# Attention on one core: minima, block copy and fill eviction shifted at unit ends

## The chip, the core and the metric

The kernel runs on one core of a Trainium2 chip. The metric is the device time of one execution in microseconds (us); the median of several runs is compared. TensorE is called PE here, VectorE DVE, ScalarE ACT, GpSimd POOL, and SP is the engine whose queue issues the DMAs.

## The reference

```python
def reference(A_x, A_wqkv, A_wo, B_x, B_w_r, B_w_gate, B_w_up, B_w_down, gate_w):
    x = A_x                                    # 1 x 2048 x 512, fp32
    g = _sigmoid((x * gate_w).sum(-1, keepdims=True))
    # a: softmax attention, 32 heads of 16, all 2048 keys for each query
    qkv = (x @ wqkv) ...                       # q, k, v: 32 x 2048 x 16
    p = _softmax(einsum("bhqd,bhkd->bhqk", q, k) * 16 ** -0.5)
    a = einsum("bhqk,bhkd->bhqd", p, v) ... @ wo
    # b: the two tokens with the largest x @ w_r pass a SwiGLU of width 1792, are scaled by
    # sigmoid of their score and added to x; all other tokens stay
    b = x + upd
    return g * a + (1 - g) * b
```

Almost all of the time goes to attention: 32 x 2048 x 2048 scores, an exponential of each, and the product of the exponentials with V.

## The kernel before

**Units.** The work is cut into 32 units. A unit is two heads and 1024 queries (the last four: four heads and 512 queries). Its scores are computed transposed, 128 keys at a time: 16 steps of four pieces, `s_piece`, each a matmul of 128 keys by 512 queries into a bank of the ring `st` (three banks), followed by an exponential on ACT into the tile `P`. Two steps later `av_mm` multiplies `P[s]` with V (the "P V" of a step, `A` in the order) and accumulates the unit's block in one PSUM bank, `av`. That bank exists once. After a unit's sixteenth step `av_out` copies it to SBUF (tile `o`, on ACT, line 670), and SP sends it off in eight DMAs.

**Maxima.** The softmax needs each query's maximum over all keys ahead of its scores. So PE computes the scores a second time, some 21 steps earlier, with queries on partitions: `m_piece`, 64 pieces for a unit, each a matmul (line 576). DVE reduces them (line 580). Of three successive pieces the first two share the two-bank tile `mxa` and one reduction, and the third has `mxb`; each tile exists once, so PE can fill one only after DVE has reduced what stood in it. When a unit's 64 pieces are reduced, `m_unit` forms the minima of its negated maxima on DVE (tile `m`, line 623), POOL splits them into a high and a low part (`hl`, lines 77 and 78), and behind the next two-bank reduction `m_rows` transposes `hl` on DVE (`hr`, line 634) and sends it in eight small DMAs into two rows of the unit's `Qx`, where the score matmuls pick it up.

**Order.** Every engine works its instructions in the order in which the program issues them, and the order is written out by hand. A pattern covers three steps:

```python
ORDER = "sssmmA smssmmA msssmmf smssmmAm".replace(" ", "")
```

`s` is a piece of scores, `m` a piece of maxima, `A` a step's P V, and `f` a fill: one piece of other work for PE from a generator (projections of later heads' q and k, the SwiGLU, the output projection), collected in a bank `fl`. A fill's PSUM result isn't copied at once: it is put on the list `late`, and `run_late` empties the list at the start of the next pattern. Evictions of projections (`evict`, tile `pe`, line 188) are copied by ACT and then split by two POOL operations into `ev` (lines 190 and 191), which SP stores. Those of the output projection (`acc_add`, tile `w`, line 464) are added up by POOL.

A unit's 64 pieces of maxima are not a multiple of three. So the last piece of a unit u falls on the second piece of `mxa` where u % 3 is 1, on the first where u % 3 is 0 (it is reduced together with the next unit's first piece), and on `mxb` where u % 3 is 2. In the first two cases the minima follow a two-bank reduction, in the third a one-bank reduction. A pattern is three steps and a unit sixteen, so the P V of a unit's last step is the last `A` of a pattern where u % 3 is 0, the first where it is 1, and the second where it is 2.

**Small operations.** Other small DVE operations are queued in `gaps`, and unit minima that await their transpose in `turn`. Behind each two-bank reduction `m_piece` takes one thing, a transpose first.

Of the kernel before, what the change touches and what calls it, by code (L numbers as in the profile page):

```python
# [11 lines left out]
AF = mybir.ActivationFunctionType  # L12
# [8 lines left out]
UNITS = PAIRS * 2  # L21
KT = S // 128
VW = DH + 1
LEAD = 21
STEPS = UNITS * KT
EL = 64
# [10 lines left out]
def gated_mix(ctx: ExitStack, tc: tile.TileContext, xT, x, wqkv, wo, w_rg, w_gate, w_up, w_down,  # L37
              consts, pos, out):
    nc = tc.nc
# [10 lines left out]
    def st_tile(shape=(128, 512)):  # L50
        return psum.tile(list(shape), F32, tag="st", name="st", bufs=3)
# [4 lines left out]
    def mxa_tile():  # L56
        return psum.tile([128, 2, 512], F32, tag="mxa", name="mxa", bufs=1)

    def mxb_tile(shape=(128, 512)):
        return psum.tile(list(shape), F32, tag="mxb", name="mxb", bufs=1)  # L60
# [4 lines left out]
    def o_tile(name, shape, dt=F32):  # L65
        return ring.tile(shape, dt, tag="o", name=name, bufs=6)
# [9 lines left out]
    def pool_split(hi, lo, src):  # L76
        nc.gpsimd.tensor_scalar(hi, src, 1.0, None, op0=OP.mult)  # L77
        nc.gpsimd.tensor_sub(lo, src, hi.bitcast(F32))
# [102 lines left out]
    def run_late():  # L181
        for f, a in late:
            f(*a)
        late.clear()
# [77 lines left out]
    def k_of(u, c):  # L262

        return Kx[(u // 2) % 2 if u < QU else 2 * c]
# [299 lines left out]
    MX, P, AV = {}, {}, {}  # L564

    def m_piece(g):

        u, e = divmod(g, EL)
        t, c, j = e // 8, e // 2 % 4, e % 2
        r = g % 3  # L570
        if r == 0:
            MX[0] = mxa_tile()
        elif r == 2:
            MX[1] = mxb_tile()
        dst = MX[0][:, r] if r < 2 else MX[1]
        nc.tensor.matmul(dst, Qx[u % 3][64 * j:64 * j + 48, t * 128:t * 128 + 128],  # L576
                         k_of(u, t // 4)[64 * j:64 * j + 48, c * 512:c * 512 + 512], start=True, stop=True)
        if r:
            g0 = (g - 1 if r == 1 else g) % (3 * EL)
            nc.vector.tensor_reduce(Mr[:, g0:g0 + (2 if r == 1 else 1)], MX[r - 1], axis=AX.X, op=OP.max, negate=True)  # L580
            if r == 1:

                if turn:
                    m_rows(*turn.pop())
                elif e > 1 and e < EL - 1 and gaps:
                    gaps.pop(0)()
            if e == EL - 1 or (e == 0 and r == 1 and g):
                m_unit(u if e else u - 1)
                if u == UNITS - 1 and e:
                    m_rows(*turn.pop())  # L590
# [30 lines left out]
    def m_unit(u):  # L621
        m = ring.tile([128, 2, 8], F32, tag="m", name="m", bufs=2)
        nc.vector.tensor_reduce(m, Mr[:, EL * (u % 3):EL * (u % 3) + EL].rearrange("p (t c j) -> p j t c", c=4, j=2),  # L623
                                axis=AX.X, op=OP.min)
        hl = ring.tile([128, 2, 2, 8], F32R, tag="hl", name="hl", bufs=2)
        pool_split(hl[:, :, 0], hl[:, :, 1], m)
        turn.append((u, hl))

    turn, gaps = [], []

    def m_rows(u, hl):

        r = ring.tile([128, 32], F32R, tag="hr", name="hr", bufs=2)
        nc.vector.transpose(r.bitcast(F32), hl.rearrange("p j i t -> p (j i t)").bitcast(F32))
        for j in range(2):
            for b in range(4):
                q = Qx[u % 3][64 * j + 48:64 * j + 50, :].rearrange("i (t n) -> i t n", n=128)
                p0 = 32 * b + 16 * j
                nc.sync.dma_start(q[:, :, 32 * b:32 * b + 32].bitcast(F32), r[p0:p0 + 16, :].bitcast(F32))

    def s_piece(s, j, c):
        u, kt = divmod(s, KT)
        if s not in P:
            P[s] = ring.tile([128, 4, 512], F32, tag="P", name="P", bufs=3)
        k = k_of(u, c)[64 * j:64 * j + 50, kt * 128:kt * 128 + 128]
        q = Qx[u % 3][64 * j:64 * j + 50, c * 512:c * 512 + 512]
        ps = mxb_tile() if s > STEPS - LEAD and c == 1 and j == 0 else st_tile()
        nc.tensor.matmul(ps, k, q, start=True, stop=True)  # L648
        nc.scalar.activation(P[s][:, 2 * j + c, :], ps, AF.Exp)  # L649

    def av_mm(s):
        u, kt = divmod(s, KT)
        if kt == 0:
            AV[0] = av_tile()
        for ct in range(4):
            h = (u // 2 * 2 if u < QU else H - 4 + ct % 2 * 2) + ct // 2
            nc.tensor.matmul(AV[0][32 * ct:32 * ct + 32, :], V[:, kt, h * VW:h * VW + 32], P[s][:, ct, :],  # L657
                             start=kt == 0, stop=kt == KT - 1)
        del P[s]
# [1 line left out]
    Lt = {}  # L661

    def av_out(u):
        pair, half = divmod(u, 2)
        g, pp = divmod(pair, 4)
        o = o_tile("o", [128, 512])
        if STEPS > u * KT + KT + 2 > STEPS - LEAD:
            nc.vector.tensor_copy(o, AV[0])
        else:
            nc.scalar.activation(o, AV[0], AF.Copy)  # L670
        if u >= QU:
            AV[u] = o
            if u == UNITS - 1:
                return
            Ls = AV["l", u] = ring.tile([128, 16], F32, tag="Ls", name="Ls", bufs=2)
            for ct in range(4):
                p = 64 * (ct % 2) + 32 * (ct // 2)
                nc.sync.dma_start(Ls[p:p + 32, :], o[32 * ct + 16:32 * ct + 17, :])
            half, q = divmod(u - QU, 2)
            for ct in range(4):  # L680
                r = 64 + 32 * (ct % 2) + 16 * (ct // 2)
                nc.sync.dma_start(last_n[half][r:r + 16, q * 512:q * 512 + 512], o[32 * ct:32 * ct + 16, :])
            return
        if u % 8 == 0:
            Lt[g] = ring.tile([128, 128], F32, tag="Lt", name="Lt", bufs=1)
        for ct in range(4):
            j, c = divmod(ct, 2)
            q0 = c * 512
            r = pp * 32 + j * 16
            if g < 3:  # L690
                d = a_scr[g * 128 + r:g * 128 + r + 16, half * 1024 + q0:half * 1024 + q0 + 512]
            else:
                d = last_n[half][r:r + 16, q0:q0 + 512]
            nc.sync.dma_start(d, o[32 * ct:32 * ct + 16, :])
            p = r + half * 8 + c * 4
            nc.sync.dma_start(Lt[g][p:p + 4, :], o[32 * ct + 16:32 * ct + 17, :])
# [78 lines left out]
    def end_step(s):  # L775
        now[0] = s
        for f, a in fill.pop(s, []):
            f(*a)
# [113 lines left out]
    def start_step(s):  # L892
        now[0] = s
        u = s // KT + 2
        if s % KT == 0 and u < UNITS:
            if u % 2 == 0 and 2 < u <= QU:
                load_k(u // 2)
            load_q(u)

    count = dict(s=0, m=0, A=-2)  # L900

    def m_next():
        if count["m"] < UNITS * EL:
            m_piece(count["m"])
            count["m"] += 1
# [3 lines left out]
    def parts_next(n):  # L909
        for _ in range(n):  # L910
            next(parts, None)
# [9 lines left out]
    count["m"] = 4 * LEAD  # L921

    while count["m"] < UNITS * EL:
        run_late()
        for o in ORDER:
            if o == "s":
                s, i = divmod(count["s"], 4)
                if i == 0:
                    start_step(s)
                s_piece(s, i % 2, i // 2)  # L930
                count["s"] += 1
                if i == 3:
                    end_step(s)
            elif o == "m":
                m_next()
            elif o == "A":
                if count["A"] < 0:
                    parts_next(3)
                p_v(count["A"])
                count["A"] += 1  # L940
            else:
                next(fills, None)
    for s in range(count["s"] // 4, STEPS + 2):
        run_late()
        if s < STEPS:
            start_step(s)
            for i in range(4):
                s_piece(s, 1 - i % 2, i // 2)
        p_v(s - 2)
        next(fills, None)  # L950
        end_step(s)
# [34 lines left out]
```

## Time and profile before

| | |
|---|---|
| three runs, median (lowest to highest) | 1433.41 us (1433.03 to 1433.73) |
| the profiled execution: its own time | 1430.75 us |
| its span, first to last instruction | 1428.9 us |
| granted PE clock, of full speed | 0.999 |
| PE busy | 1417.6 us, 99% |
| DVE busy | 1292.6 us, 90% |
| ACT busy | 1169.4 us, 82% |
| POOL busy | 312.9 us, 22% |
| exponentials, `P<-st` (ACT, line 649) | 2028 of 599 ns |
| two-bank reductions (DVE, line 580) | 655 of 1216 ns |
| one-bank reductions (DVE, line 580) | 654 of 689 ns |

The profile is of one execution, whose own time is 1430.75 us; the span leaves out 1.85 us around it. Busy time of PE is modelled: a matmul's end is not observed, so a short wait of PE can look busy. A row of the timeline reads: start in us, duration in us, engine, line, operation, tile written <- tiles read, with partitions x elements, and the count of instructions merged into the row. Square brackets give the engine's idle time before the row and what ended it.

### The profile page before, as it was taken

Reading aid. Unit: us, or ns where it says so; the run is one execution under the profiler, and the core shown is the slowest. Engines: PE = TensorE matmul, PEld = TensorE weight load, DVE = VectorE, ACT = ScalarE, POOL = GpSimd, SP = SyncE. Lnnn points to the kernel's source line nnn. Section 1 sums busy time; section 2 is a strip of 40 time slices with the busy share of each in tenths; the row PEclk is TensorE's granted clock in tenths of the full one; section 3 lists DMA queues with packets and bytes.
Section 4 is the critical chain, followed back from the end, with each engine's and each line's share of the span. In section 5 each row is a group of like instructions: output and inputs, shape, how many; then the busy total and the mean of one; then the engine's idle time right before and its main releaser. Section 6 shows DMA issues by size and latency. Waiting matters only on the chain.

```text
span 1428.9 us, 24152 instructions
## 1 busy us (share of the span) xinstructions
PE 1417.6 (99%) x9113; PEld 628.9 (44%) x9113; DVE 1292.6 (90%) x1534; ACT 1169.4 (82%) x2262; POOL 312.9 (22%) x329
## 2 busy tenths in 40 slices
PE   9999999999999999999999999999999999999998
PEld 6654444444444444444444443434444444444433
DVE  5879999999999999999999999999999999999942
ACT  4468888888888888888888888888888888888886
POOL 3661100112000001200000100032742322234500
PEclk9999999999999999999999999999999999999999
DMA  8611021212214121312222332414313031012012
GB/s 261 183 56 49 20 53 31 54 45 43 53 52 109 62 53 31 68 29 57 65 82 53 85 84 77 106 41 134 83 31 68 21 77 35 15 31 58 17 50 78
DMA packets 55096, 92.87 MB, mean 65 GB/s; under 512 B 14208, under 2 KB 25472, under 8 KB 53476
## 3 DMA queue, kind: packets, MB, share of 16 engines
q1 hardware_dynamic: 54884, 91.32, 24.7%
q8 instruction: 72, 1.18, 0.4%
q14 instruction: 44, 0.36, 0.1%
q0 software_dynamic: 96, 0.01, 0.0%
HBM read 63.77 MB, written 28.57 MB: 65 GB/s over the span
## 4 chain that ended last, share of the span: by engine, by line
PE 97%; DMA 2%; SPq 0%; DVE 0%; ACT 0%; issue 0%; ACTq 0%; DVEq 0%
PE av L657 36%; PE st L648 24%; PE mxa L576 12%; PE mxb L576 10%; PE fl L154 6%; PE fl L498 4%; PE st L283 3%; DMA xs<-xT 1%; PE mxa L607 1%; DMA wvs<-wqkv 1%; PE fl L389 0%; PE st L154 0%; DMA k_scr<-Qx 0%; PE fl L427 0%; ACT P L649 0%; DVE acc L549 0%
## 5 line engine op out<-in xcount | busy, mean ns | idle before, releaser
L649 ACT ACTIVATE P<-st 128x512 f32<-128x512 f32 x2028 | 1064.4, 599 | 200.7 <-PE st L648 108.8
L580 DVE TENSOR_REDUCE Mr<-mxa 128x2 f32<-128x1024 f32 x655 | 796.6, 1216 | 3.9 <-PE mxa L576 3.0
L657 PE MATMUL av<-P,V 128*32 128x512 f32 x4096 | 545.3, 605 | 0.0
L648 PE MATMUL st<-Qx,Kx 50*128 50x512 f32 x2028 | 537.5, 443 | 1.8 <-ACT P L649 1.8
L580 DVE TENSOR_REDUCE Mr<-mxb 128x1 f32<-128x512 f32 x654 | 450.9, 689 | 62.6 <-PE st L648 20.6
L648 PEld LDWEIGHTS st<-Qx,Kx 50*128 50x128 f32 x2028 | 276.7, 184 | 232.3 <-ACT P L649 213.4
L576 PE MATMUL mxb<-Kx,Qx 48*128 48x512 f32 x654 | 325.3, 497 | 0.0
L576 PE MATMUL mxa<-Kx,Qx 48*128 48x512 f32 x1310 | 296.0, 418 | 0.0
L576 PEld LDWEIGHTS mxb<-Kx,Qx 48*128 48x128 f32 x654 | 119.5, 183 | 273.7 <-DVE Mr L580 271.2
L576 PEld LDWEIGHTS mxa<-Kx,Qx 48*128 48x128 f32 x1310 | 124.9, 183 | 46.5 <-DVE Mr L580 5.4
L657 PEld LDWEIGHTS av<-P,V 128*32 128x32 f32 x4096 | 81.1, 108 | 141.5 <-issue 135.3
L77 POOL TENSOR_SCALAR hl<-m 128x16 fp32r<-128x16 f32 x32 | 8.1, 255 | 434.3 <-DVE m L623 434.3
L190 POOL TENSOR_SCALAR ev<-pe 128x512 fp32r<-128x512 f32 x24 | 35.8, 1492 | 299.0 <-ACT pe L188 299.0
L465 POOL TENSOR_TENSOR acc<-acc,w 128x512 f32<-128x512 f32 x32 | 41.0, 1281 | 166.7 <-ACT w L464 152.4
L154 PE MATMUL fl<-xh,wh 128*128 128x512 f32 x96 | 42.9, 447 | 0.0
L154 PE MATMUL fl<-xh,wl 128*128 128x512 f32 x96 | 40.4, 421 | 0.0
L549 DVE SCALAR_TENSOR_TENSOR acc<-fl,gg,acc 128x512 f32<-128x512 f32 x16 | 12.0, 748 | 26.3 <-PE fl L498 24.1
L498 PE MATMUL fl<-woh,ahl 128*128 128x512 f32 x96 | 35.1, 447 | 0.0
L612 DVE TENSOR_REDUCE Mr<-mxa 128x2 f32<-128x1024 f32 x21 | 25.7, 1223 | 8.2 <-PE mxa L607 8.2
L154 PE MATMUL fl<-xl,wh 128*128 128x512 f32 x96 | 32.6, 420 | 0.0
L191 POOL TENSOR_TENSOR ev<-pe,ev 128x512 fp32r<-128x512 f32 x24 | 30.9, 1286 | 2.0
L319 ACT ACTIVATE p<-p 128x512 f32<-128x512 f32 x32 | 20.0, 628 | 11.1 <-POOL p L315 10.9
(173 smaller groups left out, 765.0 us busy)
## 6 DMA issues: line engine op xcount, KB each, us to landing
Kx<-k_scr SPq DMA_DIRECT2D x30, 256.0 KB
k_scr<-ev SPq DMA_DIRECT2D x14, 512.0 KB
q_scr<-ev SPq DMA_DIRECT2D x14, 512.0 KB
Qx<-q_scr SPq DMA_DIRECT2D x54, 128.0 KB
Qx<-q_scr SPq DMA_DIRECT2D x70, 64.0 KB
xs<-xT SPq DMA_DIRECT2D x16, 256.0 KB
xn<-x SPq DMA_DIRECT2D x4, 1024.0 KB
Qx<-hr SPq DMA_DIRECT2D x256, 2.0 KB
```

Source lines behind the costliest of these rows:

```text
L154: nc.tensor.matmul(ps, a[:, i, c, :], b[nb][:, c, :], start=n == 0, stop=n == 11)
L190: nc.gpsimd.tensor_scalar(ev[:, 0], t, 1.0, None, op0=OP.mult)
L191: nc.gpsimd.tensor_sub(ev[:, 1], t, ev[:, 0].bitcast(F32))
L283: nc.tensor.matmul(ps, a[nb][:, c, sl], b[:, c, :], start=c == 0 and n == 0, stop=c == 3 and n == 2)
L465: nc.gpsimd.tensor_add(a, a, w)
L498: nc.tensor.matmul(ps, a[:, sl], b[:a.shape[0], c, :], start=first and n == 0, stop=last and n == 2)
L576: nc.tensor.matmul(dst, Qx[u % 3][64 * j:64 * j + 48, t * 128:t * 128 + 128], k_of(u, t // 4)[64 * j:64 * j + 48, c * 512:c * 512 + 512], ...
L580: nc.vector.tensor_reduce(Mr[:, g0:g0 + (2 if r == 1 else 1)], MX[r - 1], axis=AX.X, op=OP.max, negate=True)
L612: nc.vector.tensor_reduce(*r, axis=AX.X, op=OP.max, negate=True)
L648: nc.tensor.matmul(ps, k, q, start=True, stop=True)
L649: nc.scalar.activation(P[s][:, 2 * j + c, :], ps, AF.Exp)
L657: nc.tensor.matmul(AV[0][32 * ct:32 * ct + 32, :], V[:, kt, h * VW:h * VW + 32], P[s][:, ct, :], start=kt == 0, stop=kt == KT - 1)
```

## The change

Three things are moved; no arithmetic is added or taken away.

- Where a unit's last piece of maxima is a one-bank piece (u % 3 = 2), its minima wait in a list `due` and are issued behind the next two-bank reduction. Their transpose then follows one two-bank reduction later.
- Where the last P V of a unit is the second `A` of its pattern (u % 3 = 2, up to unit 29), the copy of its block is made in two halves of 256 columns: the first at once, the second after three more pieces of scores. The DMAs of the block follow the second half.
- Where a unit has ended with the last `A` of a pattern (u % 3 = 0), `run_late` is called after the first `A` of the next pattern and not at its start.

```diff
@@ m_piece
             if r == 1:
-                if turn:
+                if due:
+                    m_unit(due.pop())
+                elif turn:
                     m_rows(*turn.pop())
                 elif e > 1 and e < EL - 1 and gaps:
                     gaps.pop(0)()
-            if e == EL - 1 or (e == 0 and r == 1 and g):
+            if e == EL - 1 and r == 2 and u < UNITS - 1:
+                due.append(u)
+            elif e == EL - 1 or (e == 0 and r == 1 and g):
                 m_unit(u if e else u - 1)
@@ s_piece
         nc.scalar.activation(P[s][:, 2 * j + c, :], ps, AF.Exp)
+        o_half()
@@ av_out
         if STEPS > u * KT + KT + 2 > STEPS - LEAD:
             nc.vector.tensor_copy(o, AV[0])
+        elif STEPS - LEAD > u * KT + KT + 2 and u % 3 == 2:
+            nc.scalar.activation(o[:, :256], AV[0][:, :256], AF.Copy)
+            half_o.append([3, u, o, AV[0]])
+            return
         else:
             nc.scalar.activation(o, AV[0], AF.Copy)
+        o_rows(u, o)
+
+    half_o = []
+
+    def o_half():
+        if half_o:
+            half_o[0][0] -= 1
+            if not half_o[0][0]:
+                _, u, o, ps = half_o.pop()
+                nc.scalar.activation(o[:, 256:], ps[:, 256:], AF.Copy)
+                o_rows(u, o)
+
+    def o_rows(u, o):               # what av_out did behind its copy: the DMAs of the block
+        pair, half = divmod(u, 2)
+        g, pp = divmod(pair, 4)
@@ the loop over patterns
     while count["m"] < UNITS * EL:
-        run_late()
+        hold = count["A"] % KT == 0 and count["A"] > 0
+        if not hold:
+            run_late()
         for o in ORDER:
...
                 p_v(count["A"])
                 count["A"] += 1
+                if hold:
+                    hold = False
+                    run_late()
```

More of the change, by code (lines that the diff above doesn't have):

```diff
@@ L627, in m_unit @@
         turn.append((u, hl))
-    turn, gaps = [], []
+    due, turn, gaps = [], [], []
     def m_rows(u, hl):
@@ L663, in av_out @@
     def av_out(u):
-        pair, half = divmod(u, 2)
-        g, pp = divmod(pair, 4)
         o = o_tile("o", [128, 512])
```

## The prediction

> **What bounds the kernel.** First the page: the busy shares, and the chain of waits by engine.
>
> ```profile
> PE 1417.6 (99%) x9113; PEld 628.9 (44%) x9113; DVE 1292.6 (90%) x1534; ACT 1169.4 (82%) x2262; POOL 312.9 (22%) x329
> ...
> PE 97%; DMA 2%; SPq 0%; DVE 0%; ACT 0%; issue 0%; ACTq 0%; DVEq 0%
> ```
>
> The chain is PE's, but a PE that waits a tenth of a microsecond for a neighbour looks busy here. So next I read the timeline, pattern by pattern of ORDER (numbered from 0; twelve scores, twelve maxima, three P V, one fill). Three units take 16 patterns, so each unit end stands at a fixed place: a unit with u % 3 = 2 ends its maxima with the last `m` of a pattern and its P V with the second `A`; one with u % 3 = 0 ends its P V with the last `A`. PE's first maximum matmul of patterns 8, 9, 10, and of the last end of this kind:
>
> ```profile
> 159.27 0.49 PE L576 MATMUL mxb<-Kx,Qx 48*128 48x512 f32 x1
> ...
> 166.97 0.50 PE L576 MATMUL mxb<-Kx,Qx 48*128 48x512 f32 x1
> ...
> 174.91 0.49 PE L576 MATMUL mxb<-Kx,Qx 48*128 48x512 f32 x1
> ...
> 1282.41 0.50 PE L576 MATMUL mxb<-Kx,Qx 48*128 48x512 f32 x1
> ...
> 1290.34 0.50 PE L576 MATMUL mxb<-Kx,Qx 48*128 48x512 f32 x1
> ```
>
> An ordinary pattern takes 7.70 us (159.27 to 166.97); the one that opens with the minima of unit 2 takes 7.94, that of unit 29 takes 7.93. There are ten such ends (units 2, 5, ... 29), with 0.24 us lost at the first and 0.23 at the last. Why, VectorE's timeline around unit 8 shows, with PE's P V groups:
>
> ```profile
> 409.42 0.69 DVE L580 TENSOR_REDUCE Mr<-mxb 128x1 f32<-128x512 f32 x1
> ...
> 411.36 0.69 DVE L580 TENSOR_REDUCE Mr<-mxb 128x1 f32<-128x512 f32 x1
> 411.97 1.22 DVE L580 TENSOR_REDUCE Mr<-mxa 128x2 f32<-128x1024 f32 x1
> 413.20 0.69 DVE L580 TENSOR_REDUCE Mr<-mxb 128x1 f32<-128x512 f32 x1
> ...
> 415.22 0.69 DVE L580 TENSOR_REDUCE Mr<-mxb 128x1 f32<-128x512 f32 x1 [0.19 <-PE st L648]
> 415.94 0.22 DVE L623 TENSOR_REDUCE m<-Mr 128x16 f32<-128x64 f32 x1
> 416.09 1.20 DVE L580 TENSOR_REDUCE Mr<-mxa 128x2 f32<-128x1024 f32 x1
> 417.23 0.19 DVE L634 STREAM_TRANSPOSE hr<-hl 128x32 f32<-128x32 f32 x1
> 417.35 0.64 DVE L580 TENSOR_REDUCE Mr<-mxb 128x1 f32<-128x512 f32 x1
> ```
>
> ```profile
> 407.86 1.07 PE L657 MATMUL av<-P,V 128*32 128x512 f32 x8
> ...
> 409.82 1.07 PE L657 MATMUL av<-P,V 128*32 128x512 f32 x8
> ...
> 413.69 1.07 PE L657 MATMUL av<-P,V 128*32 128x512 f32 x8
> ...
> 415.59 1.07 PE L657 MATMUL av<-P,V 128*32 128x512 f32 x8
> ...
> 417.77 1.07 PE L657 MATMUL av<-P,V 128*32 128x512 f32 x8
> ```
>
> From one P V group to the next is 1.96 in an ordinary pattern (407.86 to 409.82), here 2.18 (415.59 to 417.77). VectorE's two-bank reduction normally starts 0.61 after the one-bank reduction in front of it (411.36 to 411.97); with the minima between, 0.87 (415.22 to 416.09). It ends at 417.29 rather than 417.05, and PE, which needs the two banks `mxa` again, waits. VectorE has little to spare: idle before a one-bank reduction in most groups, but none in the last group (411.97 + 1.22 = 413.19, the next starts at 413.20).
>
> **Minima behind the two-bank reduction.** Nothing is added or removed: ten times the 0.22 us reduction L623 goes one place on, and the transpose L634 with its eight row DMAs two reductions on. What a small operation costs depends on whether it waits for the one just ahead. The minima do today: 0.87 - 0.61 = 0.26. The transpose does not: it starts at 417.23, before the reduction ends (417.29), and the next follows at 417.35, so it costs 0.06. In the changed order the minima need columns that the reduction before last wrote, so 0.06 is the nearest row; the ends are 0.06 and 0.26.
>
> Replayed at unit 8: the two-bank reduction starts at 415.22 + 0.61 = 415.83 and ends at 417.05; VectorE is free at 417.11. The one-bank reduction comes ordinarily 1.56 after the P V group (409.42 - 407.86), that is 417.15: the minima vanish in idle time. The next P V group is at 415.59 + 1.96 = 417.55. The next two-bank reduction runs from 417.76 to 418.98, the transpose frees VectorE at 419.04, and the following one-bank reduction is due 1.54 after that group (411.36 - 409.82), at 419.09: hidden too. What is late next is PE itself, at its own 7.70. A queued small operation of `gaps` goes one slot on, no more. I take a gain of 0.22 where the whole loss is there.
>
> It isn't at every second of these ends. Units 6, 12, 18, 24 begin a new pair of heads, so a new K tile, and PE is late by itself ahead of the minima. Unit 11's end:
>
> ```profile
> 539.58 1.07 PE L657 MATMUL av<-P,V 128*32 128x512 f32 x8
> ...
> 541.64 1.06 PE L657 MATMUL av<-P,V 128*32 128x512 f32 x8
> ```
>
> Between its groups lie 2.06, only 0.10 over 1.96. So six ends give 0.22 and four 0.11: 1.32 + 0.44 = 1.8 us. The bounds are 1.2 (rival 1) and 2.4 (ten whole losses).
>
> ScalarE's eviction of a fill feeds two POOL operations that now stand ahead of the unit's high/low split `hl`, at four ends (units 8, 11, 14, 17); the transpose, and all of VectorE behind it, waits for `hl`:
>
> ```profile
> 414.61 0.62 ACT L188 ACTIVATE pe<-fl 128x512 f32<-128x512 f32 x1
> ...
> 416.25 0.25 POOL L77 TENSOR_SCALAR hl<-m 128x16 fp32r<-128x16 f32 x1 [28.94 <-DVE m L623]
> ...
> 416.78 1.49 POOL L190 TENSOR_SCALAR ev<-pe 128x512 fp32r<-128x512 f32 x1
> 418.35 1.28 POOL L191 TENSOR_TENSOR ev<-pe,ev 128x512 fp32r<-128x512 f32 x1
> ```
>
> The pair takes 2.85 (416.78 to 419.63), the split 0.53 (416.25 to 416.78). The evicted tile is ready at 415.23, so the pair ends near 418.1 and the split by 418.7; the transpose wants it at 418.9: covered, with 0.2 to spare. SP keeps its order; the row DMAs go out some 1.9 later at the ends without an eviction. Issue of these rows, and the group whose third score is the unit's first, at unit 17 and at unit 20:
>
> ```profile
> 792.10 5.27 SPq L639 DMA_DIRECT2D Qx<-hr  x8
> ...
> 798.09 0.73 PE L648 MATMUL st<-Qx,Kx 50*128 50x512 f32 x3
> ...
> 912.92 5.27 SPq L639 DMA_DIRECT2D Qx<-hr  x8
> ...
> 921.96 0.73 PE L648 MATMUL st<-Qx,Kx 50*128 50x512 f32 x3
> ```
>
> Unit 20 has 3.8 from the end of issue (918.19) to that group, and keeps 1.9; unit 17 gets by with 0.7 today, so nothing is due. At units 8 to 17 the rows stand on SP behind the evicted tile's store, which now comes earlier.
>
> **The copy in halves.** Ten copies of 128x512 (units 2 to 29) become twenty of 128x256, three exponentials apart; the eight DMAs behind each go out those three exponentials later, to readers patterns away. Today the whole copy sits ahead of the second group's scores. Second to third P V of the first and the last of these patterns:
>
> ```profile
> 224.16 1.06 PE L657 MATMUL av<-P,V 128*32 128x512 f32 x8
> ...
> 228.13 1.07 PE L657 MATMUL av<-P,V 128*32 128x512 f32 x8
> ...
> 1339.49 1.07 PE L657 MATMUL av<-P,V 128*32 128x512 f32 x8
> ...
> 1343.44 1.07 PE L657 MATMUL av<-P,V 128*32 128x512 f32 x8
> ```
>
> That is 3.97 and 3.95 against 3.87 ordinarily (409.82 to 413.69): 0.10 and 0.08 lost. The first half falls into ScalarE's idle time before that group, the second after the fill, where a pause stands too. The eight between lose less than these two; I take 10 x 0.07 = 0.7, from 0 (a half costs as much as a whole, and the second one does the harm) to 0.9. The next unit's first P V needs the bank empty: it stands behind the last group's scores, whose exponentials come after the second half, so the copy is out of its way.
>
> **Eviction one step on.** By the order of instructions only two ScalarE evictions move, at the ends of units 18 (a 112-row sliver) and 27. Unit 27's pattern, and below it the same place without an eviction:
>
> ```profile
> 1258.60 0.50 PE L576 MATMUL mxb<-Kx,Qx 48*128 48x512 f32 x1
> ...
> 1259.29 0.68 ACT L464 ACTIVATE w<-fl,gg 128x512 f32<-128x512 f32 x1
> ...
> 1267.01 0.50 PE L576 MATMUL mxb<-Kx,Qx 48*128 48x512 f32 x1
> ```
>
> ```profile
> 515.31 0.50 PE L576 MATMUL mxb<-Kx,Qx 48*128 48x512 f32 x1
> ...
> 523.15 0.50 PE L576 MATMUL mxb<-Kx,Qx 48*128 48x512 f32 x1
> ```
>
> 8.41 against 7.84: the eviction straight behind the block copy costs 0.57. Three exponentials later it meets a ScalarE that has caught up; I take 0.6 for both places, from 0.3 (half comes back) to 0.7.
>
> **Sum.** 1.8 + 0.7 + 0.6 = 3.1 us less, all of it on PE's chain, so the end moves with it. The profiled execution took 1430.75 (span 1428.9): it becomes 1427.65. The runs' median, 1433.41, is 2.66 above that execution; I carry the difference: 1430.3. My terms' bounds give gains of 2.0 to 4.0: 1429.4 to 1431.4. A measurement of this kernel can tell 0.2%, 2.87 us, from no change: the bar is 1430.54, and the forecast lies barely past it.
>
> **Rivals.**
> 1. The minima keep their price of 0.26 in the new place. Then VectorE is free at 417.31 rather than 417.15, the lag is 0.11 after the transpose, and in the last group, which has no idle time, PE waits 0.10. The six ends give 0.12, the four 0.11: 1.2, in all 2.5: 1430.9. For it: the minima do carry a wait. Against: the transpose's early start. The Trainium skill (VectorE: DVE Perf Modes, "The DRAIN you can't avoid") speaks for this one: the pipe empties after every vector operation, and leaving out the wait between two saves nothing. By that rule the time is this rival's; the transpose that starts 0.06 before its predecessor ends disagrees.
> 2. The first move does nothing: what is lost is the first read of the next unit's tiles, as at unit 11. Then 0.7 + 0.6 = 1.3: 1432.1. Against it: the 0.87 for 0.61 on VectorE at unit 8.
> 3. Slower: the split `hl` comes late behind the eviction pair, the transpose waits, and VectorE and PE with it. It decides from 0.2 us of further lateness; were POOL late by another such pair, 2.85, each of the four ends would lose 2.65, 10.6 in all, less the 3.1: 1440.9. For it: the margin is thin. Against: in these rows POOL stood idle for 28.94 us before.
>
> **Chances.** Forecast 0.62, rival 1 0.17, rival 2 0.13, rival 3 0.08. The range, 1429.4 to 1432.2, holds the first three but for the edges of their terms. Faster by over 0.2%: three quarters of the forecast and a third of rival 1, 0.52. Within: the rest of both, and rival 2, 0.40. Slower: 0.08.
>
> **What would show it.** Right: patterns such as unit 2's at 7.72 and unit 11's at about 7.82, the minima starting before the two-bank reduction ends, second to third P V at 3.88 where the copy is halved, unit 27's pattern at 7.85. Wrong: a last group 0.1 longer at these ends (rival 1), 2.18 still between the groups at unit 8 (rival 2), VectorE idle ahead of the transpose with POOL as releaser (rival 3), or PE waiting for `o` at the next unit's first P V.

## The result and the profile after

| | before | after |
|---|---|---|
| median of 11 runs (lowest to highest) | 1433.20 us (1431.57 to 1433.73) | 1429.59 us (1428.40 to 1432.07) |
| after over before, 95% interval | | 0.9978 (0.9969 to 0.9986) |
| the profiled execution, its own time (span) | 1430.75 us (1428.9) | 1432.07 us (1430.3) |
| of it: up to the start of pattern 1 / patterns 1 to 161 / behind them | 105.0 / 1247.18 / 76.7 us | 108.5 / 1243.51 / 78.3 us |

The change saves 3.6 us by the medians. The two profiled executions say the opposite, and have to be cut up before they can be compared: the last row does it, by the starts of one maximum matmul per pattern in the timeline of PE. It is the one just ahead of the pattern, the last `m` of the pattern before; the prediction calls it the pattern's first, and counted from that one the loop is shorter by the same 3.67. In the 1247 us that the change touches, the changed kernel is 3.67 us faster. It lost 3.5 us before pattern 1 and 1.6 behind the last, where the change does nothing. Stretches of the startup, of before and then of after (stretch, its length, busy time of PE, PEld, DVE, ACT and POOL with instruction counts, granted PE clock, DMA share, GB/s):

```profile
26.00:33.00 7.00, 6.18 (x18) 4.03 (x18) 3.79 (x5) 1.20 (x3) 2.16 (x2) 0.76 0.69 185
33.00:40.00 7.00, 7.00 (x31) 4.95 (x32) 5.01 (x7) 0.81 (x2) 0.00 (x0) 1.00 0.90 200
```

```profile
26.00:33.00 7.00, 4.22 (x17) 2.83 (x17) 3.55 (x4) 1.42 (x3) 2.43 (x2) 1.00 0.76 198
33.00:40.00 7.00, 7.00 (x20) 4.58 (x17) 3.08 (x5) 0.55 (x1) 0.00 (x0) 0.51 0.92 196
```

While the first inputs come in, PE's clock falls to half for a time that differs from execution to execution: here 3.4 us of it in before (26.7 to 30.2) and 6.8 in after (33.0 to 39.8). The drop alone does not set the length of the startup: a later run with the same 6.8 us (the third part alone) reached pattern 1 at 106.5, and one without a drop there (minima that wait) at 105.9. So everything below compares patterns, not spans.

The page of the profile hardly moves (busy shares, and the chain of waits by engine):

```profile
PE 1416.9 (99%) x9113; PEld 633.2 (44%) x9113; DVE 1292.0 (90%) x1534; ACT 1169.0 (82%) x2272; POOL 313.2 (22%) x329
...
PE 97%; DMA 1%; SPq 1%; ACT 0%; DVE 0%; issue 0%; ACTq 0%; DVEq 0%
```

PE is modelled as 99% busy in both: a loss of 0.2 us a pattern doesn't show here, only in the timeline. The maximum matmul of PE from which patterns 8, 9, 10 of the changed kernel are counted:

```profile
162.74 0.50 PE L576 MATMUL mxb<-Kx,Qx 48*128 48x512 f32 x1
...
170.44 0.50 PE L576 MATMUL mxb<-Kx,Qx 48*128 48x512 f32 x1
...
178.13 0.50 PE L576 MATMUL mxb<-Kx,Qx 48*128 48x512 f32 x1
```

7.70 and 7.69: the pattern with unit 2's minima is an ordinary one now (it was 7.94). DVE's timeline around unit 8, POOL's beside it, and PE's P V groups:

```profile
418.11 0.69 DVE L580 TENSOR_REDUCE Mr<-mxb 128x1 f32<-128x512 f32 x1 [0.16 <-PE st L652]
418.72 1.22 DVE L580 TENSOR_REDUCE Mr<-mxa 128x2 f32<-128x1024 f32 x1
419.85 0.21 DVE L627 TENSOR_REDUCE m<-Mr 128x16 f32<-128x64 f32 x1
420.06 0.69 DVE L580 TENSOR_REDUCE Mr<-mxb 128x1 f32<-128x512 f32 x1
...
421.80 0.20 DVE L638 STREAM_TRANSPOSE hr<-hl 128x32 f32<-128x32 f32 x1
```

```profile
418.24 1.49 POOL L190 TENSOR_SCALAR ev<-pe 128x512 fp32r<-128x512 f32 x1 [28.00 <-ACT pe L188]
419.81 1.29 POOL L191 TENSOR_TENSOR ev<-pe,ev 128x512 fp32r<-128x512 f32 x1
...
421.41 0.22 POOL L78 TENSOR_TENSOR hl<-m,hl 128x16 fp32r<-128x16 f32 x1
```

```profile
416.58 1.07 PE L662 MATMUL av<-P,V 128*32 128x512 f32 x8
418.50 1.06 PE L662 MATMUL av<-P,V 128*32 128x512 f32 x8
420.44 1.06 PE L662 MATMUL av<-P,V 128*32 128x512 f32 x8
```

The minima start at 419.85, 0.09 before the two-bank reduction ends (419.94). The two-bank reduction in front of them starts 0.61 after its predecessor (418.11 to 418.72; it was 0.87), and the P V group comes 1.94 after the one before (it was 2.18). The POOL order is the one foreseen: the eviction's pair ahead of the split, which ends at 421.63, and the transpose goes at 421.80.

The copy in halves, ACT and PE, at the first place:

```profile
227.43 1.07 PE L662 MATMUL av<-P,V 128*32 128x512 f32 x8
...
228.62 0.39 ACT L673 ACTIVATE o<-av 128x256 f32<-128x256 f32 x1
...
230.44 0.40 ACT L688 ACTIVATE o<-av 128x256 f32<-128x256 f32 x1
...
231.29 1.07 PE L662 MATMUL av<-P,V 128*32 128x512 f32 x8
```

3.86 from the second to the third P V (it was 3.97). And unit 27's pattern, PE:

```profile
1259.16 0.50 PE L576 MATMUL mxb<-Kx,Qx 48*128 48x512 f32 x1
...
1267.00 0.50 PE L576 MATMUL mxb<-Kx,Qx 48*128 48x512 f32 x1
...
1274.79 0.50 PE L576 MATMUL mxb<-Kx,Qx 48*128 48x512 f32 x1
```

7.84 (it was 8.41), and 7.79 for the pattern behind. Summed over the loop, by place, each pattern against the same pattern of before:

| | patterns | before, each | after, each | sum |
|---|---|---|---|---|
| minima, units 2, 5, ... 29 | 10 | 7.93 to 7.95 | 7.69 to 7.72 (six), 7.75 to 7.82 (four) | -2.10 us |
| copy in halves | 10 | 7.76 to 7.82 | 7.69 to 7.74 | -0.75 us |
| eviction, units 18 and 27 | 2 | 7.92, 8.41 | 7.82, 7.85 | -0.67 us |
| the pattern behind unit 27's | 1 | 7.70 | 7.79 | +0.09 us |

These make 3.43 of the 3.67; the other 138 patterns hold the rest, none of them by more than 0.06. That rest is not shown to be an effect: in the runs of the three parts below the same 138 patterns sum to between -0.04 and +0.24 against before.

### The profile page after: what moved, and what is told of

Read it like the earlier page. It is cut to its first block, busy times and chain, and to the rows that moved or that the text cites. A ratio compares the mean times of both kernels' runs of the same rounds, so it can differ in the third digit from the quotient of the medians.

```text
span 1430.3 us, 24162 instructions
## 1 busy us (share of the span) xinstructions
PE 1416.9 (99%) x9113; PEld 633.2 (44%) x9113; DVE 1292.0 (90%) x1534; ACT 1169.0 (82%) x2272; POOL 313.2 (22%) x329
## 4 chain that ended last, share of the span: by engine, by line
PE 97%; DMA 1%; SPq 1%; ACT 0%; DVE 0%; issue 0%; ACTq 0%; DVEq 0%
PE av L662 36%; PE st L652 23%; PE mxa L576 12%; PE mxb L576 10%; PE fl L154 6%; PE fl L498 4%; PE st L283 3%; DMA xs<-xT 1%; PE mxa L611 1%; DMA wvs<-wqkv 1%; PE fl L389 0%; PE st L154 0%; PE fl L427 0%; ACT P L653 0%; SPq L202 0%; PE st L788 0%
## 5 line engine op out<-in xcount | busy, mean ns | idle before, releaser
L653 ACT ACTIVATE P<-st 128x512 f32<-128x512 f32 x2028 | 1064.7, 598 | 196.3 <-PE st L652 108.5
L285 ACT ACTIVATE V<-st 128x512 f32<-128x512 f32 x16 | 9.6, 600 | 28.1 <-PE st L283 28.1
```

## Experiments

**Each part alone.** To the kernel before, one of the three parts is applied, as in the diff: `due` (first run), the halves (second), `hold` (third).

> The minima behind the two-bank reduction, alone. If the three moves are independent, only the ten patterns that open at an end of a unit with u % 3 = 2 change: from 7.94 to 7.70 (units 2, 8, 14, 20, 26, 29) and 7.76 (units 5, 11, 23; unit 17 7.82), and patterns 1 to 162 take 2.1 us less than the 1247.18 of before; the median falls by about as much, ratio 0.9985. The ten patterns with the block copy stay at 7.79 on average and unit 27's at 8.41. If the moves lean on each other, the gain at these ends is not that of the full change.

> The copy in halves, alone. Independent: the ten patterns with the block copy at the second P V go from 7.79 on average to 7.71, patterns 1 to 162 lose 0.75 us, all other patterns stay within 0.03. If a half costs as much as a whole and the second half does the harm, they stay at 7.79.

> The eviction one step on, alone. Two patterns change: that of unit 18's end from 7.92 to 7.82 and that of unit 27's end from 8.41 to 7.85, together 0.66 us; nothing else over 0.03. The rival, that the eviction is late there for the matmuls behind it, gives back some of it in the pattern after.

By the same places: the first part gives -2.18 at the ten minima patterns; the second -0.74 at the ten copy patterns, all at 7.69 to 7.73; the third -0.10 at unit 18 and -0.58 at unit 27, with +0.12 in the pattern behind. Each acts only at its own places, and -2.18 - 0.74 - 0.56 = -3.48 against 3.43 in the full change: they add up. Over the whole loop the three gain 1.94, 0.74 and 0.39, 3.07 in all against 3.67, for the other patterns drift by some 0.2 from execution to execution.

Whole times resolve little of this: the first part, timed in five rounds, had a median of 1431.08 (11 runs) against 1432.15 for before on that chip (15 runs), ratio 0.999 (0.998 to 0.9999); the one execution of the second took 1431.20 and that of the third 1433.08, within what startup and tail vary.

**Is it the wait that costs? Minima that wait for the reduction just ahead.** The changed kernel, but `m` reads the columns of the next unit, which the two-bank reduction in front of it has just written:

```diff
-                    m_unit(due.pop())
+                    m_unit(due.pop(), 1)
-    def m_unit(u):
+    def m_unit(u, ahead=0):
+        v = (u + ahead) % 3          # and Mr's columns of v in place of u % 3
```

> The full change, but the ten minima are taken over the next unit's columns, two of which the two-bank reduction just ahead has written, so they must wait for that reduction (the minima used are therefore not the right ones). If the price of a small operation lies in waiting for its predecessor, it starts 0.03 after the reduction's end and no longer 0.09 before it, VectorE is 0.1 to 0.2 later, and the odd ends go from 7.70 to between 7.72 and 7.80, 0.1 to 1.0 us in all. If only the place counts, the ends stay at 7.70 and 7.76.

DVE's timeline at unit 8:

```profile
416.56 1.21 DVE L580 TENSOR_REDUCE Mr<-mxa 128x2 f32<-128x1024 f32 x1
417.80 0.22 DVE L628 TENSOR_REDUCE m<-Mr 128x16 f32<-128x64 f32 x1
418.12 0.69 DVE L580 TENSOR_REDUCE Mr<-mxb 128x1 f32<-128x512 f32 x1
```

The minima start 0.03 after the reduction's end (417.77) and the next reduction 0.35 after it, against 0.12 in the changed kernel (419.94 to 420.06). The pattern takes 7.84; all ten take 7.83 to 7.85, above the 7.72 to 7.80 that I had expected. So half of the gain goes: -1.04 in place of -2.10. By end it is 0.12 to 0.14 at six and 0.02 to 0.08 at the four that begin a new K tile, all of it between the second and the third P V, the last group that rival 1 names.

But the edit adds more than the wait that it was made for. These minima read all 64 columns of the next unit, and the next reduction writes one of them, so it has to wait for the minima in turn. The trace has it wait for DVE's own semaphore beside PE's at these ten places, and it starts 0.10 after the minima's end (418.02 to 418.12). What the first wait costs without the second, the ends of the other units show, whose minima follow a two-bank reduction and need its columns. Unit 4's in the changed kernel:

```profile
252.69 1.22 DVE L580 TENSOR_REDUCE Mr<-mxa 128x2 f32<-128x1024 f32 x1
253.94 0.22 DVE L627 TENSOR_REDUCE m<-Mr 128x16 f32<-128x64 f32 x1
254.08 0.68 DVE L580 TENSOR_REDUCE Mr<-mxb 128x1 f32<-128x512 f32 x1
```

The minima start 0.03 after the reduction's end (253.91), and the next reduction 0.17 after it, before the minima are done. In the changed kernel the next reduction starts 0.10 to 0.13 after that end at the six ends with the whole loss, and 0.21 to 0.23 after it at the four, each time about 1.56 after a P V group, where an ordinary one-bank reduction starts too. An estimate from these rows: the wait alone would make DVE late by 0.04 to 0.07 at six ends and at none of the four, and cost at most 0.3 us in all. Most of the 1.06 lost would then be the second wait's. A run that has the first wait alone at these ends was not made, so this is argued.

**What remains at the minima: leave them out.** The kernel before, with the ten reductions L623 of units 2, 5, ... 29 left out; 16 columns of `Mr` are split in their place.

```diff
...
+        if u % 3 == 2:
+            m = Mr[:, EL * (u % 3) + 48:EL * (u % 3) + 64].rearrange("p (j t) -> p j t", j=2)
...
```

> The kernel before without its ten minima reductions at the ends of units with u % 3 = 2: POOL splits sixteen of the unit's negated maxima in their place (the reduction is left out), the transpose stays where it was. If the minima are what is lost there, these patterns fall from 7.94 to about 7.70 and to 7.76 at the ends before a new K tile, 2.1 us in all. If it is the first read of the next unit's tiles, they stay near 7.94.

PE at unit 8:

```profile
414.79 0.50 PE L576 MATMUL mxb<-Kx,Qx 48*128 48x512 f32 x1
...
422.50 0.49 PE L576 MATMUL mxb<-Kx,Qx 48*128 48x512 f32 x1
```

7.71, and over the ten -2.15, against -2.10 where they are moved: minima in the new place cost nothing that can be seen. Units 5, 11, 17 and 23 keep 7.74 to 7.77 even without them, so what is left there isn't the minima's.

**Rival 3's threshold: a later split.** The changed kernel, but POOL makes the split once more at units 8 and 11, three times more at 14 and 17 (the same values each time).

```diff
-        pool_split(hl[:, :, 0], hl[:, :, 1], m)
+        for _ in range(1 + {8: 1, 11: 1, 14: 3, 17: 3}.get(u, 0)):
+            pool_split(hl[:, :, 0], hl[:, :, 1], m)
```

> The full change with the high/low split repeated on POOL, which makes it later at the four ends where an eviction stands ahead of it: once more at units 8 and 11 (0.57 us later), three times more at units 14 and 17 (1.7 us later). By the prediction's third rival the cover is some 0.2 us, then the transpose stalls VectorE and PE: about 0.3 us lost at units 8 and 11 and about 1.4 at units 14 and 17, 3.4 in all. If VectorE and PE have more to give than these 0.2, units 8 and 11 show nothing and units 14 and 17 below 1.2.

At units 8 and 11 the patterns took 8.12 and 8.10, +0.42 and +0.35 for a split about 0.57 later: a margin of some 0.2, as the prediction had it (the changed kernel's own rows show 0.17). At unit 17 it was 9.38, +1.56. Unit 14 lost more: 10.56 (+2.87), and its next pattern 9.46 (+1.76). DVE's timeline there, and the stretches around it (columns as above):

```profile
668.58 0.21 DVE L639 STREAM_TRANSPOSE hr<-hl 128x32 f32<-128x32 f32 x1 [1.71 <-POOL hl L78]
```

```profile
668.30:670.38 2.08, 1.19 (x5) 0.44 (x4) 1.80 (x3) 1.06 (x3) 0.22 (x1) 1.00 0.23 47
671.30:674.70 3.40, 3.40 (x16) 1.00 (x14) 1.91 (x2) 0.70 (x2) 0.00 (x0) 0.50 0.02 3
674.70:677.70 3.00, 3.00 (x16) 0.91 (x14) 1.50 (x2) 1.19 (x3) 0.00 (x0) 0.58 0.81 250
```

The transpose waits 1.71 for POOL, PE starves (busy 1.19 of 2.08), and then PE's granted clock is 0.50 from 670.4 to 677.2. At unit 17 the transpose waited 1.59, and there was no such drop:

```profile
796.60:799.20 2.60, 1.65 (x7) 0.67 (x6) 2.40 (x5) 1.67 (x4) 0.17 (x1) 1.00 0.14 34
```

So the direct price of the late split is what rival 3 said, and the clock is a second one that nothing on record had foreseen: the whole loop is 7.30 longer than the changed kernel's, where 3.4 was expected.

**Cut the copy, or only move it?** The changed kernel, with the whole copy at the second half's place and none at the first:

```diff
-            nc.scalar.activation(o[:, :256], AV[0][:, :256], AF.Copy)
             half_o.append([3, u, o, AV[0]])
...
-                nc.scalar.activation(o[:, 256:], ps[:, 256:], AF.Copy)
+                nc.scalar.activation(o, ps, AF.Copy)
```

> The full change with the whole block copied where it has the second half: no split, only the place. If the gain comes from cutting the copy, so that each half falls into a pause of ScalarE, a whole copy (about 0.5 us of ScalarE) in a pause of about 0.3 makes the last group's exponentials 0.2 late, and the patterns lie between 7.71 and 7.79. If the place alone counts, they stay at 7.71. Were the next unit's first P V held up by the bank, they would be over 7.79.

PE's pattern starts at the last of these places (unit 29), and ACT's timeline in it:

```profile
1334.68 0.50 PE L576 MATMUL mxb<-Kx,Qx 48*128 48x512 f32 x1
...
1342.40 0.50 PE L576 MATMUL mxb<-Kx,Qx 48*128 48x512 f32 x1
...
1350.33 0.49 PE L576 MATMUL mxb<-Kx,Qx 48*128 48x512 f32 x1
```

```profile
1340.55 0.62 ACT L687 ACTIVATE o<-av 128x512 f32<-128x512 f32 x1
1341.03 1.61 ACT L653 ACTIVATE P<-st 128x512 f32<-128x512 f32 x3
1342.45 0.75 ACT L464 ACTIVATE w<-fl,gg 128x512 f32<-128x512 f32 x1
```

7.72 and then 7.93, where before has 7.78 for the second: the copy's own patterns gain as much as with halves (-0.75 over ten, 7.70 to 7.73 each), and the patterns behind give back 0.74, which no branch of the expectation had. At unit 29 ACT is late into the next pattern, whose eviction is first. Moving alone gains nothing; two pieces that each fit into a pause do.

**Every end one step on?** The changed kernel, with all of a unit's minima (also those that follow a two-bank reduction already) one reduction later:

```diff
-            if e == EL - 1 and r == 2 and u < UNITS - 1:
-                due.append(u)
+            if u < UNITS - 1 and e == EL - 1 or (e == 0 and r == 1 and g):
+                due.append(u if e else u - 1)
```

> The full change, and the minima of the other units also one two-bank reduction later, so that no minima wait for the reduction just ahead. Their ends cost little today (7.71 and 7.73 at u % 3 = 1, two patterns; 7.82 at u % 3 = 0, of which the trace puts the most on first reads of a new unit's tiles). If the wait is a price only where VectorE has no idle time, nothing changes by over 0.3 us in all; if it is a price everywhere, some 0.1 comes back at each of twenty ends, 2 us.

Two patterns became longer, those that need the rows of units 1 and 4, by 1.05 and 1.17; the others stayed within 0.07, and without these two the loop is 0.12 shorter than the changed kernel's. SP's issues for unit 4, in the changed kernel and in this one, and PE in this one:

```profile
256.04 5.28 SPq L643 DMA_DIRECT2D Qx<-hr  x8
261.42 0.39 SPq L176 DMA_DIRECT2D k_scr<-ev  x1
```

```profile
258.15 0.38 SPq L176 DMA_DIRECT2D k_scr<-ev  x1
258.62 5.30 SPq L643 DMA_DIRECT2D Qx<-hr  x8
```

```profile
265.24 0.47 PE L652 MATMUL st<-Qx,Kx 50*128 50x512 f32 x1 [0.75 <-DMA Qx<-hr]
```

The rows are issued 3.8 later (2.6 on the two time axes, and this execution's pattern 20 starts 1.2 earlier), behind the store, and PE waits for them until 265.24, 1.3 after the last issue ended (263.92). The change itself moves only the u % 3 = 2 ends, which have this room.

This run also settles what the wait is worth at the other ends, for here no minima wait for the reduction just ahead. Unit 15's:

```profile
708.29 1.22 DVE L580 TENSOR_REDUCE Mr<-mxa 128x2 f32<-128x1024 f32 x1
709.43 0.21 DVE L627 TENSOR_REDUCE m<-Mr 128x16 f32<-128x64 f32 x1
709.55 0.68 DVE L580 TENSOR_REDUCE Mr<-mxb 128x1 f32<-128x512 f32 x1
```

The next reduction starts 0.04 after the end of the one ahead (709.51), where unit 4's above, with the wait, has 0.17. That is 0.13 us of DVE at an end, and PE hardly feels it: the 0.12 above is all that the loop shows for some twenty ends, as in the first branch of the expectation.

**The other copies: part of them on DVE.** Patterns with the copy of a u % 3 = 0 unit still take 7.76 to 7.85. The changed kernel, with 256 of their 512 columns copied by DVE, and then 128:

```diff
+        elif STEPS - LEAD > u * KT + KT + 2 and u % 3 == 0:
+            nc.scalar.activation(o[:, :256], AV[0][:, :256], AF.Copy)      # 384 in the second
+            nc.vector.tensor_copy(o[:, 256:], AV[0][:, 256:])
```

> The full change, and at the ends of units with u % 3 = 0 ScalarE copies the first 256 columns of the block and VectorE the other 256. Ten patterns that open behind this copy take 7.82 on average because the copy makes ScalarE's first exponential about 0.15 late. If VectorE's idle time of some 0.15 ahead of the first one-bank reduction covers its half, they fall to 7.72, 1.0 us in all. If VectorE is what counts, its half (about 0.3) makes the two-bank reduction late and they stay at 7.82 or rise to 7.95.

> As before, but ScalarE copies 384 columns and VectorE 128. ScalarE's copy is then about 0.1 shorter and VectorE's part about 0.2. By the first view the ten patterns fall to about 7.75, 0.7 us in all; by the second they stay between 7.80 and 7.85.

Both are worse: 8.03 to 8.11 and 8.01 to 8.10 at these ten places. That is longer than either branch of the expectations. DVE's timeline of the first at unit 12:

```profile
516.67 0.42 DVE L678 COPY o<-av 128x256 f32<-128x256 f32 x1 [0.26 <-ACT o L677]
```

DVE's copy doesn't run beside ACT's: it waits for it (by the rows of this line, 2.3 us in nine places; the smaller copy 3.6 in ten), and everything behind it on DVE with it. The smaller copy waits longer, since ACT's part is larger. Why a copy of other columns waits for ACT wasn't taken apart. No version here beats the change.

## Why the prediction was right

The direction, the sum and the places were right: 3.1 us forecast, 3.61 by the medians, 3.43 by the places. Step by step:

- **Minima: 1.8 forecast, 2.10 measured.** The reading that they vanish held (leaving them out gives -2.15). The six ends with the whole loss gave 0.24 each (0.22 forecast). That a small operation's price depends on whether it waits for the one just ahead held only in part. The wait is worth 0.13 on DVE, half of the 0.26 at the old place. But minima that do wait, behind a two-bank reduction, cost PE some 0.02 an end (units 1, 4, ... 28 in the changed kernel: 7.69 to 7.73, and 7.73 on average in the pattern behind, which has 7.70 where nothing waits). So what frees the ten is in the main their place: the one-bank reduction behind them starts when PE is ready, the two-bank reduction behind the old place as soon as DVE is free. No run has them at the old place without the wait, so how much each counts there is argued.
- **The mis-sized term is the four ends at a new K tile:** 0.11 each forecast, 0.17 measured. I set the second group's 2.06 at unit 11 against 1.96 of an ordinary pattern. But the 1.96 contains a wait for DVE itself. PE's P V groups around unit 11, before (with the two rows shown in the prediction) and after:

```profile
537.55 1.07 PE L657 MATMUL av<-P,V 128*32 128x512 f32 x8
```

```profile
540.11 1.07 PE L662 MATMUL av<-P,V 128*32 128x512 f32 x8
542.12 1.06 PE L662 MATMUL av<-P,V 128*32 128x512 f32 x8
544.01 1.07 PE L662 MATMUL av<-P,V 128*32 128x512 f32 x8
```

Before: 2.03 and 2.06. After: 2.01 and 1.89, where unit 8 has 1.92 and 1.94. The first group is late at unit 11 with or without minima. DVE uses that lateness to catch up, and then PE runs the second group at its own pace, 1.89. It is so at all four such ends (1.89 to 1.90, and 1.89 to 1.91 where the minima are left out), while the other six have 1.94 to 1.97. The loss was 2.06 - 1.89 = 0.17 there, not 0.10.
- **Halves: 0.7 forecast, 0.75 measured.** 3.86 where 3.88 was expected. The reason held too: each half fits a pause of ACT, while the whole copy in the second place gives back what it gains.
- **Eviction: 0.6 forecast, 0.58 net measured** (-0.67, and 0.09 given back in the pattern behind unit 27's, which the prediction didn't name).
- **Rival 1** has a real cost and overprices it. The 0.26 is counted from a start 0.08 ahead of the predecessor's end (0.61 behind the start of a reduction of 0.69), but the prediction adds it to the end, while its 0.06 for the transpose is counted from the end. From the end, minima that wait hold the next reduction up for 0.17 and those that don't for 0.04, so VectorE would be free at 417.05 + 0.17 = 417.22 and not at 417.31. The rule of the Trainium skill beside it (VectorE: DVE Perf Modes, "The DRAIN you can't avoid"), by which leaving out the wait between two operations saves nothing, disagrees with the trace: the next reduction started 0.17 after the one ahead with the minima's wait and 0.04 without it. The same section of the Trainium skill adds that a next operation that is not held starts earlier; the trace agrees, 0.08 to 0.09 before the end.
- **Rival 2** falls: without the minima the ten patterns are short, so the loss was theirs. The first read of a new unit's tiles is left as 0.05 to 0.12 at four ends; that it is this read is only argued.
- **Rival 3** has its threshold where the prediction put it, at about 0.2 us. In the changed kernel the split makes it with 0.17 to spare. Its price at a lateness beyond that was too low by the clock.
- **The range:** the terms' own lower bounds, 1.2, 0 and 0.3, add up to 1.5, not to the 2.0 that the prediction gives; nothing came out that low.
- **The carry from one profiled execution to the median** held by luck: startup and tail differ by 5 us between the two profiled executions, more than the whole change.

## What to carry to other kernels

What a small operation costs depends on where it stands: ahead of a step that starts as soon as its engine is free, it cost up to 0.24 us a pattern here; one step later, ahead of a step that starts when another engine is ready, nothing. That it waits for its direct predecessor is a price on its own engine (0.13 us), of which little may reach the engine that bounds the kernel. And an edit that adds a wait can add a second one behind it: look at what the next instruction waits for before you price the first. An ordinary interval isn't an engine's own pace until you have seen it run shorter; and work moved into a pause has to be small enough to fit it, or the next stage pays.

## What the runs showed of the hardware

- PE's granted clock fell to 0.50 for 6.8 us (670.4 to 677.2) after a stretch in which PE was still busy 1.19 of 2.08 us; after one with 1.65 of 2.60 it stayed at 1.00. The startup shows the same kind of drop: 4.22 busy of 7.0, then 0.51 granted for 7 us. A wait of 1.71 us on DVE cost 4.63 us with the drop (2.87 and 1.76, two patterns), one of 1.59 cost 1.56 without it. Why the one stall draws the drop and the other doesn't is open.
- An operation of DVE that depends on its predecessor started 0.03 after that one's end, an independent one 0.06 to 0.09 before it. The next reduction started 0.17 and 0.04 after the same end, and 0.35 where it had to wait for the small operation itself.
- Halving an ACT copy of 512 PSUM columns takes 0.39 to 0.40 for each half against 0.62 for the whole. DVE needs 0.42 for 256 columns and 0.29 for 128.
- Eight small DMAs cost SP 5.3 us of issue, and a score matmul that had waited for their rows started 1.3 us after the last issue ended.
